# One whole transpose for the ninth key block, in place of two 64-row pieces

## The chip, the cores and the metric

One core of a Trainium2 chip runs the whole kernel. The metric is device time in microseconds (us) of one execution; of several runs the median is taken. The engines named below are TensorE (PE in the profile, with its weight loads as PEld), VectorE (DVE), ScalarE (ACT), GpSimd (POOL) and SyncE (SP), which issues the transfers.

## What is computed

Attention with queries pooled by two, then two feed-forward layers over the 1152 rows that it leaves. The change is in the attention alone. All data is float32.

```python
q_pool = q.reshape(B, H, S // 2, 2, D).mean(axis=3)       # B 2, H 8, S 1152, D 64
scores = D ** -0.5 * q_pool @ k.transpose(0, 1, 3, 2)     # 576 queries x 1152 keys
attn = exp(scores - max) / (sum + 1e-9)
x = (attn @ v)                                            # -> 1152 rows x 512
x = moe(x)        # x @ w_in, a rational function, @ w_out
out = moe2(x)     # RMS norm, silu gate, value, @ w_out
```

## The kernel before

**Tiles.** A pair of heads has 2 x 576 queries, cut into nine tiles of 128 queries (the fifth holds 64 of each head). Eight pairs give 72 tiles. A tile's scores are 128 queries by 1152 keys in one PSUM tile of three banks (`hid`; there are two of them, taken in turn: even tiles have one, odd tiles the other). Banks 0 and 1 hold 512 keys each, bank 2 the last 128, the ninth key block.

**A tile's steps.** TensorE computes the scores (line 782): `AB` is the part in banks 0 and 1, `C` the part in bank 2. VectorE takes the row maximum (line 811), ScalarE the exponential into `p` in SBUF (line 817). TensorE transposes `p` back into the same three banks (line 833), in pieces of 64 queries by 128 keys that use 64 rows of the array: pieces of queries 0 to 63 go to bank 0, those of queries 64 to 127 to bank 1, so that the two halves of the array work side by side. Three copies bring the banks to `pt` in SBUF (line 865 where ScalarE does it, 868 where VectorE does). Then `av` multiplies `pt` by the values (line 937). The scores of the tile after next need the same banks, so `AB` waits for the copies of banks 0 and 1, and `C` for that of bank 2.

**The ninth block.** It belongs in bank 2 for both halves. The piece of the upper queries goes there first, ahead of the other 16 pieces (`f_T`, 17 pieces). The piece of the lower queries is an operation of its own, `T2` (`f_T2`), which waits for the copy of bank 0; only after it is bank 2 copied.

**The other work in this stretch.** TensorE also transposes the next heads' `k` and `q` (`prep`, line 730) and the reciprocal sums (`rx`, lines 970 and 984), which take the whole 128 x 128 array. VectorE, ScalarE and GpSimd copy those results out, and prepare the weights of the feed-forward layers (`wc`, `wraw`, `spill`).

**Order.** Every step is an `Op` with a cost in ns. A list scheduler, `order`, writes the program from these costs, the keys and the dependencies, and chooses the engine of a step that may run on several (`op_any`). On TensorE the attention's steps are held in a row written by hand, `seq`: for tiles a and b of a couple it was AB(a), T2 of the couple before's b, C(a), AB(b), C(b), five steps of `av`, T(a), T(b), T2(a). `prep` and `rx` are put in between by the scheduler. The costs say 560 for `T` and 60 for `T2`; switching between row pieces, column pieces and the whole array is charged 100 between steps.

Of the kernel before, what the change touches and what calls it, by code (L numbers as in the profile page):

```python
# [19 lines left out]
def attention_moe_moe2_kernel(  # L20
# [18 lines left out]
    nc = tc.nc  # L39
    B, H, S, D = q.shape  # L40
# [25 lines left out]
    def T(tag, shape, dtype=F32, space=None):  # L66
        pool(tag, BUFS.get(tag, 1), space)
        return pools[tag].tile(shape, dtype, tag=tag, name=tag)
# [7 lines left out]
    ident = T("ident", [128, 128])  # L76
# [367 lines left out]
    PE, DVE, ACT, POOL = "PE", "DVE", "ACT", "POOL"  # L444
# [86 lines left out]

    after = mybir.DependencyInfo(mybir.DependencyClass.Sync, mybir.DependencyReason.DATA)

    def banked(accesses, g, ins, also=None):

        ins = ins.ins
        for o in range(3):
            for other in accesses[o]:
                if other.engine != ins.engine:
                    if o != g and other is not also:  # L540
                        tc.declare_no_dep(ins, other, reason="another bank")
                    else:
                        tc.add_manual_dep(ins, other.name, after, reason="the same bank")
        accesses[g].append(ins)
# [7 lines left out]
    def bank_access(w, u, c, ins):  # L552
        if w == "in" and u in FINE or (w, u) in (("gate", 0), ("val", NU2 - 1)):
            banked(hid_bank.setdefault((w, u), [[] for _ in range(NC)]), c, ins)
# [71 lines left out]
    def op_any(ways, key, deps=(), bufs=()):  # L626
        eng, c, fn = ways[0]
        return Op(eng, c, key, fn, deps, bufs, ways[1:])
# [7 lines left out]
    bank = [[[] for _ in range(3)] for _ in range(2)]  # L636
# [123 lines left out]
    pt, pt_buf, pt_op, sums, sum_buf, sum_op, xt_ops, xt_buf, x_op = ({} for _ in range(9))  # L760

    def tile_ops(i):
        pr, t = divmod(i, NT)
        parts, dests = TILES[t]
        ps = s_ps[i % 2]
        key = i * TS
        e = {}
        nb, pb = Buf("nm"), Buf("p")
        if t == 0:
            sum_buf[pr] = Buf("sums")  # L770
        sb = sum_buf[pr]


        ORDER_QK = [[(1, 1, 0, 256), (0, 0, 0, 256), (1, 1, 256, 512), (0, 0, 256, 512)], [(0, 2, 512, 640)]]

        def f_qk(n_):
            fresh = {}
            for a, j, x0, x1 in ORDER_QK[n_]:
                rows = slice(64 * a, 64 * a + 64)
                c = x0 % 512  # L780
                for h, c0, to in parts:
                    ins = nc.tensor.matmul(  # L782
                        ps[to, j, c:c + x1 - x0],
                        lhsT=qT[2 * pr + h][rows, c0:c0 + to.stop - to.start],
                        rhs=kT[2 * pr + h][rows, x0:x1],
                        start=True,
                        stop=True,
                    )
                    banked(bank[i % 2], j, ins)
                    fresh.setdefault(j, []).append(ins.ins)  # L790
            for j in fresh:
                bank[i % 2][j][:] = fresh[j]

        deps, bufs = [], []
        for h, c0, to in parts:
            deps += kT_op[2 * pr + h]
            deps += [o for (x0, x1), o in qT_op[2 * pr + h] if x0 < c0 + to.stop - to.start and x1 > c0]
            bufs += kq_buf[2 * pr + h]
        o_qk = []
        for n_, (js, c) in enumerate((((0, 1), 870), ((2,), 220))):  # L800
            free = [o for j in js for o in lo_op.get((i - 2, j), ())]
            o_qk.append(Op(PE, c, key + n_, lambda n_=n_: f_qk(n_), [*deps, *free], bufs))
            o_qk[-1].mode = "rows"
        tile_pe[i] = {"AB": o_qk[0], "C": o_qk[1]}

        def scores():
            return ps.rearrange("p g n -> p (g n)")[:, 0:S]

        def f_red():
            e["nm"] = T("nm", [128, 1])  # L810
            nc.vector.tensor_reduce(out=e["nm"], in_=scores(), op=ALU.max, axis=AX.X, negate=True)  # L811

        def f_exp():
            if pr not in sums:
                sums[pr] = T("sums", [128, NT])
            e["p"] = T("p", [128, S])
            nc.scalar.activation(  # L817
                e["p"], scores(), AF.Exp, bias=e["nm"], scale=1.0, accum_out=sums[pr][:, t:t + 1]
            )

        o_red = Op(DVE, 1350, key + -2500, f_red, o_qk, [nb])
        o_exp = Op(ACT, 1430, key + 2400, f_exp, [o_red], [nb, pb, sb])
        o_red.chain = o_exp.chain = True
        sum_op.setdefault(pr, []).append(o_exp)

        NB = NKT - 1

        def one_T(r, j, also=None):  # L830
            g, c = (2, 64 * r) if j == NB else (r, 64 * j)
            rows = slice(64 * r, 64 * r + 64)
            ins = nc.tensor.transpose(ps[:, g, c:c + 64], e["p"][rows, 128 * j:128 * j + 128], ident[rows, rows])  # L833
            banked(bank[i % 2], g, ins, also)

        def f_T():
            one_T(1, NB)
            for j in range(NB):
                one_T(0, j)
                one_T(1, j)  # L840

        def f_T2():
            one_T(0, NB, e["copied"].ins)


        OUTS = [(0, slice(0, NB), 0), (1, slice(0, NB), 1), (2, slice(NB, NKT), None)]

        def f_out(n_, copy):
            g, js, half = OUTS[n_]
            src = ps[:, g, 0:64 * NB if half is not None else 128]  # L850
            for h, o, s0, n in dests:
                if (pr, h) not in pt:
                    pt[pr, h] = T("pt", [128, NKT, SQ])
                to = pt[pr, h][:, js]
                if half is None:
                    banked(bank[i % 2], g, copy(to[:, 0, o:o + n], src[:, s0:s0 + n]))
                elif s0 <= 64 * half < s0 + n:
                    o_ = o + 64 * half - s0
                    ins = copy(to[:, :, o_:o_ + 64], src.rearrange("p (j n) -> p j n", n=64))
                    banked(bank[i % 2], g, ins)  # L860
                    if g == 0:
                        e["copied"] = ins

        def by_act(to, src):
            return nc.scalar.activation(to, src, AF.Copy)  # L865

        def by_dve(to, src):
            return nc.vector.tensor_copy(to, src)  # L868

        o_T = Op(PE, 560, key, f_T, [o_exp], [pb])  # L870
        o_T.mode = "rows"
        for h, *_ in dests:
            if (pr, h) not in pt_buf:
                pt_buf[pr, h] = Buf("pt")
        for n_ in range(3):
            half = OUTS[n_][2]
            hs = [h for h, o, s0, n in dests if half is None or s0 <= 64 * half < s0 + n]
            w = 64 * NB if half is not None else 128
            n2 = 150 * (len(hs) - 1)
            done = op_any(  # L880
                [(ACT, 70 + 1.09 * w + n2, lambda n_=n_: f_out(n_, by_act)), (DVE, 80 + 1.16 * w + n2, lambda n_=n_: f_out(n_, by_dve))],
                key + 3300 + 300 * n_, [o_T if half is not None else o_T2], [pt_buf[pr, h] for h in hs],
            )
            done.chain = True
            if n_ == 0:
                o_T2 = Op(PE, 60, key + 300, f_T2, [done], [pb])
                o_T2.mode = "rows"
                tile_pe[i].update(T=o_T, T2=o_T2)
            lo_op[i, OUTS[n_][0]] = [done]
            for h in hs:  # L890
                pt_op.setdefault((pr, h), []).append(done)
# [126 lines left out]
    tile_pe, av_ops = {}, []  # L1018
    AV2 = 5

    def attention():
        Op(PE, 213 * WARM, -1e6, f_warm)
        for i in range(len(heads)):
            head_ops(i)
        for i in range(NP * NT):
            tile_ops(i)
            if i % NT == NT - 1:
                pair_ops(i // NT)


        seq = []
        n = NP * NT
        for i in range(0, n, 2):
            a, b = tile_pe[i], tile_pe[i + 1]
            was = tile_pe.get(i - 1)
            seq += [a["AB"], *([was["T2"]] if was else []), a["C"], b["AB"], b["C"]]
            for _ in range(AV2):
                if av_ops and av_ops[0][0] < i - AVLAG:
                    seq.append(av_ops.pop(0)[1])
            seq += [a["T"], b["T"], a["T2"]]  # L1040
        seq.append(tile_pe[n - 1]["T2"])
        for x, y in zip(seq, seq[1:]):
            y.deps.append(x)

# [480 lines left out]
```

## Time and profile before

| | |
|---|---|
| three runs, median (lowest to highest) | 719.26 us (718.44 to 719.62) |
| profiled execution, its span | 719.1 us |
| attention, first transpose of `p` to the feed-forward's first product | 12.0 to 269.2 us of the span |
| TensorE busy over the span | 691.1 us (96%) |
| VectorE, ScalarE, GpSimd busy | 544.7, 392.6, 262.3 us |

The profiled execution is 0.2 us under the median of the runs, so a sum in its microseconds can be read against either. The profile counts an instruction as busy from its issue to its end; matmuls overlap one another, so that a busy TensorE is not a full one, and times between starts say more than busy shares. A product of float32 operands shows as two matmuls, a transpose as one.

### The profile page before, as it was taken

The numbers are of one execution on the slowest core, as the hardware profiler recorded it, in microseconds if no ns is written. First come the engines' busy times: TensorE is split into PE (matmuls) and PEld (weight loads), VectorE is DVE, ScalarE is ACT, GpSimd is POOL, SyncE is SP. The second block draws the span as 40 slices with busy tenths as digits, with TensorE's granted clock in tenths as the row PEclk, the third lists the DMA queues.
The fourth block names the chain that finished last, engine by engine and source line by source line (L and its number), as shares of the span: only waits on it lengthen the run. The fifth ranks groups of instructions, "written<-read, shape, count | busy, mean of one in ns | idle before, by whom it ended". The sixth has DMA issues, their size and how long they took to land.

```text
span 719.1 us, 13053 instructions
## 1 busy us (share of the span) xinstructions
PE 691.1 (96%) x5257; PEld 599.5 (83%) x5257; DVE 544.7 (76%) x732; ACT 392.6 (55%) x614; POOL 262.3 (36%) x245
## 2 busy tenths in 40 slices
PE   7999999999999999899999999998999999999997
PEld 6676767767676768789999999997999899989996
DVE  5599998999889883998996967958768146845844
ACT  4566767777777774988745655344334223402210
POOL 3022355566655554222222233155345033503500
PEclk9799999999999999999999999999999999999999
DMA  7333346574644525223104104010224212420103
GB/s 214 99 117 104 115 134 202 169 233 164 223 147 155 180 103 176 89 88 118 60 30 151 55 0 147 30 31 0 88 89 139 68 58 72 134 88 29 60 1 131
DMA packets 51596, 77.13 MB, mean 107 GB/s; under 512 B 4176, under 2 KB 33872, under 8 KB 51536
## 3 DMA queue, kind: packets, MB, share of 16 engines
q1 hardware_dynamic: 51536, 76.30, 32.8%
q8 instruction: 41, 0.67, 0.4%
q14 instruction: 19, 0.16, 0.1%
HBM read 61.87 MB, written 14.42 MB: 106 GB/s over the span
## 4 chain that ended last, share of the span: by engine, by line
PE 80%; DVE 10%; ACT 3%; issue 3%; DMA 2%; POOL 1%; SPq 0%; DVEq 0%; POOLq 0%; ACTq 0%
PE hid L525 31%; PE accp L525 23%; PE hid L782 9%; PE av L937 8%; PE hid L833 5%; PE prep L730 2%; DVE pt L868 2%; DVE nm L811 2%; ACT p L817 1%; DVE acc L1323 1%; DMA wraw<-in_moe_w_gate_dram 1%; DMA wraw<-in_moe_w_out_dram 1%; DVE xt L619 1%; DVE wc L184 1%; ACT pt L865 1%
## 5 line engine op out<-in xcount | busy, mean ns | idle before, releaser
L525 PE MATMUL hid<-x_hi,win_hi 128*128 128x384 f32 x480 | 161.5, 336 | 4.5 <-DVE m_p L1133 2.3
L525 PE MATMUL hid<-x_lo,win_hi 128*128 128x384 f32 x480 | 160.7, 335 | 0.6 <-DVE x_lo L1333 0.6
L525 PE MATMUL hid<-x_hi,win_lo 128*128 128x384 f32 x480 | 160.5, 334 | 0.0
L817 ACT ACTIVATE p<-hid,nm 128x1152 f32<-128x1152 f32 x72 | 87.8, 1220 | 32.9 <-DVE nm L811 32.3
L811 DVE TENSOR_REDUCE nm<-hid 128x1 f32<-128x1152 f32 x72 | 94.9, 1353 | 9.0 <-PE hid L782 7.4
L782 PE MATMUL hid<-kT,qT 64*128 64x256 f32 (+3 forms) x800 | 99.7, 379 | 1.9 <-DVE pt L868 1.6
L525 PEld LDWEIGHTS hid<-x_hi,win_hi 128*128 128x128 f32 x480 | 90.2, 188 | 7.3 <-issue 4.5
L1175 POOL TENSOR_TENSOR g_lo<-m_p,g_hi 128x1152 fp32r<-128x1152 f32 (+1 forms) x20 | 44.9, 2252 | 134.7 <-ACT g_hi L1172 96.4
L525 PEld LDWEIGHTS hid<-x_lo,win_hi 128*128 128x128 f32 x480 | 90.1, 188 | 1.8 <-DVE x_lo L1333 0.9
L525 PEld LDWEIGHTS hid<-x_hi,win_lo 128*128 128x128 f32 x480 | 90.1, 188 | 0.0
L782 PEld LDWEIGHTS hid<-kT,qT 64*128 64x128 f32 (+1 forms) x800 | 75.5, 182 | 12.0 <-DVE pt L868 3.4
L833 PEld LDWEIGHTS hid<-ident,p 64*128 64x128 f32 x1296 | 53.4, 141 | 36.3 <-ACT p L817 13.3
L833 PE MATMUL hid<-ident,p 64*128 64x64 f32 x1296 | 67.6, 231 | 10.7 <-ACT p L817 7.2
L865 ACT ACTIVATE pt<-hid 128x512 f32<-128x512 f32 (+2 forms) x135 | 57.0, 455 | 37.6 <-PE hid L833 36.5
L937 PE MATMUL av<-pt,vn 128*64 128x288 f32 x576 | 76.7, 411 | 0.0
L525 PE MATMUL accp<-g_hi,wout_hi 128*128 128x384 f32 x192 | 64.9, 338 | 2.8 <-ACT acc L1228 1.6
L868 DVE COPY pt<-hid 128x512 f32<-128x512 f32 (+1 forms) x89 | 50.4, 584 | 19.6 <-PE hid L833 19.2
L525 PE MATMUL accp<-g_lo,wout_hi 128*128 128x384 f32 x192 | 64.4, 335 | 0.1
L525 PE MATMUL accp<-g_hi,wout_lo 128*128 128x384 f32 x192 | 64.2, 334 | 0.0
L937 PEld LDWEIGHTS av<-pt,vn 128*64 128x64 f32 x576 | 38.6, 136 | 26.9 <-issue 2.7
L175 ACT ACTIVATE wc<-wraw 128x512 f32<-128x512 f32 x68 | 45.5, 671 | 24.6 <-POOL win_lo L208 14.7
L203 POOL TENSOR_SCALAR win_hi<-wc 128x512 fp32r<-128x512 f32 x23 | 15.8, 687 | 107.6 <-PE hid L525 90.8
(121 smaller groups left out, 1231.4 us busy)
## 6 DMA issues: line engine op xcount, KB each, us to landing
wraw<-in_moe_w_out_dram SPq DMA_DIRECT2D x28, 512.0 KB, 3.5
far<-spill SPq DMA_DIRECT2D x23, 512.0 KB, 3.5
wraw<-in_moe_w_in_dram SPq DMA_DIRECT2D x16, 512.0 KB, 3.9
wraw<-in_moe_w_gate_dram SPq DMA_DIRECT2D x12, 512.0 KB, 3.5
wraw<-in_moe_w_val_dram SPq DMA_DIRECT2D x12, 512.0 KB, 4.2
kn<-in_k_dram SPq DMA_DIRECT2D x16, 288.0 KB, 3.9
vn<-in_v_dram SPq DMA_DIRECT2D x16, 288.0 KB, 3.0
qn<-in_q_dram SPq DMA_DIRECT2D x16, 256.0 KB, 3.6
```

What stands on the lines that cost most here:

```text
L175: nc.scalar.activation(c.bitcast(F32), wt["raw", n][:, :, 1].bitcast(F32), AF.Abs, scale=2.0**-112)
L203: eng.tensor_scalar(hi, w_float(n), 1.0, 1.0, op0=ALU.mult, op1=ALU.mult)
L525: ins = nc.tensor.matmul(dst, lhsT=a[x], rhs=b[y], start=first and i == 0 and p == 0, stop=last and i == n - 1 and p == 2,)
L730: seen(nc.tensor.transpose(ps[0:src.shape[1], at:at + 128], src, ident))
L782: ins = nc.tensor.matmul(ps[to, j, c:c + x1 - x0], lhsT=qT[2 * pr + h][rows, c0:c0 + to.stop - to.start], rhs=kT[2 * pr + h][rows, x0:x1], ...
L811: nc.vector.tensor_reduce(out=e["nm"], in_=scores(), op=ALU.max, axis=AX.X, negate=True)
L817: nc.scalar.activation(e["p"], scores(), AF.Exp, bias=e["nm"], scale=1.0, accum_out=sums[pr][:, t:t + 1])
L833: ins = nc.tensor.transpose(ps[:, g, c:c + 64], e["p"][rows, 128 * j:128 * j + 128], ident[rows, rows])
L865: return nc.scalar.activation(to, src, AF.Copy)
L868: return nc.vector.tensor_copy(to, src)
L937: nc.tensor.matmul(e["av", h][64 * c:64 * c + 64, 0:QW], lhsT=v_tile[2 * pr + h][:, KEYS[kt], :], rhs=pt[pr, h][:, kt, c * QW:(c + 1) * QW ...
L1175: eng.tensor_sub(g_(1), p_(), g_(0).bitcast(F32))
```

## The change

The ninth block is transposed as one 128 x 128 block into bank 2, at the head of the tile's transposes, followed by the 16 row pieces of the other blocks. `T2` is gone from the tile and from the hand-written row, and with it its wait for the copy of bank 0. `T` is now costed at 750.

```diff
-    def banked(accesses, g, ins, also=None):
+    def banked(accesses, g, ins):
...
-                    if o != g and other is not also:
+                    if o != g:
                         tc.declare_no_dep(ins, other, reason="another bank")
...
-        def one_T(r, j, also=None):
-            g, c = (2, 64 * r) if j == NB else (r, 64 * j)
-            rows = slice(64 * r, 64 * r + 64)
-            ins = nc.tensor.transpose(ps[:, g, c:c + 64], e["p"][rows, 128 * j:128 * j + 128], ident[rows, rows])
-            banked(bank[i % 2], g, ins, also)
-
         def f_T():
-            one_T(1, NB)
+            banked(bank[i % 2], 2, nc.tensor.transpose(ps[:, 2, 0:128], e["p"][:, 128 * NB:S], ident))
             for j in range(NB):
-                one_T(0, j)
-                one_T(1, j)
-
-        def f_T2():
-            one_T(0, NB, e["copied"].ins)
+                for r in range(2):
+                    rows = slice(64 * r, 64 * r + 64)
+                    ins = nc.tensor.transpose(
+                        ps[:, r, 64 * j:64 * j + 64], e["p"][rows, 128 * j:128 * j + 128], ident[rows, rows]
+                    )
+                    banked(bank[i % 2], r, ins)
...
-        o_T = Op(PE, 560, key, f_T, [o_exp], [pb])
+        o_T = tile_pe[i]["T"] = Op(PE, 750, key, f_T, [o_exp], [pb])
...
-                key + 3300 + 300 * n_, [o_T if half is not None else o_T2], [pt_buf[pr, h] for h in hs],
+                key + 3300 + 300 * n_, [o_T], [pt_buf[pr, h] for h in hs],
...
-            if n_ == 0:
-                o_T2 = Op(PE, 60, key + 300, f_T2, [done], [pb])
...
-            was = tile_pe.get(i - 1)
-            seq += [a["AB"], *([was["T2"]] if was else []), a["C"], b["AB"], b["C"]]
+            seq += [a["AB"], a["C"], b["AB"], b["C"]]
...
-            seq += [a["T"], b["T"], a["T2"]]
-        seq.append(tile_pe[n - 1]["T2"])
+            seq += [a["T"], b["T"]]
```

On TensorE, a couple of tiles late in the attention stood like this before. `hid_156` is the PSUM tile of tile a, `hid_157` that of tile b; `p_...` are their exponentials, `kT`/`qT` the operands of the scores.

```order
L937 MATMUL av_3231<-pt_2979,vn_2653 64x288 x10
L833 MATMUL hid_156<-ident_66,p_3238 128x64 x17
L833 MATMUL hid_157<-ident_66,p_3251 128x64 x17
L833 MATMUL hid_156<-ident_66,p_3238 128x64
L782 MATMUL hid_156<-kT1_2909,qT1_2947 128x256 x4
L833 MATMUL hid_157<-ident_66,p_3251 128x64
L782 MATMUL hid_156<-kT1_2909,qT1_2947 128x128
L782 MATMUL hid_157<-kT0_3148,qT0_3196 128x256 x4
L782 MATMUL hid_157<-kT0_3148,qT0_3196 128x128
L937 MATMUL av_3231<-pt_2979,vn_2653 64x288 x8
```

Now the same couple stands like this:

```order
L926 MATMUL av_3156<-pt_2944,vn_2592 64x288 x10
L831 MATMUL hid_156<-ident_66,p_3159 128x128
L835 MATMUL hid_156<-ident_66,p_3159 128x64 x16
L831 MATMUL hid_157<-ident_66,p_3174 128x128
L835 MATMUL hid_157<-ident_66,p_3174 128x64 x16
L782 MATMUL hid_156<-kT1_2838,qT1_2871 128x256 x4
L782 MATMUL hid_156<-kT1_2838,qT1_2871 128x128
L782 MATMUL hid_157<-kT0_3077,qT0_3128 128x256 x4
L782 MATMUL hid_157<-kT0_3077,qT0_3128 128x128
L926 MATMUL av_3156<-pt_2944,vn_2592 64x288 x8
```

The two single pieces (`T2`) are gone, and each run of row pieces has a whole block at its head. Over the attention the program changes 229 times between row pieces, column pieces and the whole array, where it changed 155 times; the scheduler also puts some of `prep` and `rx` elsewhere.

The scheduler divides the copies anew. On VectorE, the work between the maxima of one couple (the 25th) and the next stood like this before; `xt` is the copy of `av`'s result.

```order
L811 TENSOR_REDUCE nm_2639<-hid_157 128x1
L180 TENSOR_SCALAR wc_2614<-wc_2614 128x512
L223 SCALAR_TENSOR_TENSOR wc_2614<-wraw_2394,wc_2614 128x512
L868 COPY pt_2491<-hid_156 128x8x64
L619 TENSOR_SCALAR xt_2442<-av_2529 64x288 x2
L868 COPY pt_2491<-hid_157 128x8x64
L988 TENSOR_TENSOR xt_2442<-xt_2442,prep_2573 128x512
```

And now:

```order
L811 TENSOR_REDUCE nm_2578<-hid_157 128x1
L180 TENSOR_SCALAR wc_2553<-wc_2553 128x512
L223 SCALAR_TENSOR_TENSOR wc_2553<-wraw_2335,wc_2553 128x512
L619 TENSOR_SCALAR xt_2383<-av_2469 64x288
L861 COPY pt_2438<-hid_156 128x8x64
L861 COPY pt_2438<-hid_156 128x128
L861 COPY pt_2646<-hid_157 128x8x64
L977 TENSOR_TENSOR xt_2383<-xt_2383,prep_2537 128x512
```

One `xt` has gone to ScalarE, the other stands ahead of the copies, and bank 2 of tile a is copied between the two large copies. Over the whole program VectorE loses 5 copies of `xt`, 12 of `qT`, 4 sums of `q` (`qp`), 5 small copies of `kT`, 4 products of `xt` with `rxh` and 2 of `win_lo`; it gains one large copy of `kT` and 16 of `pt`, two of them large.

## Rows read from the trace of the kernel before

**Rows 1.** Windows: engines' busy time (instructions), granted clock, DMA share, GB/s.

```profile
12.00:269.20 257.20, 245.52 (x2793) 175.67 (x2793) 225.78 (x339) 187.44 (x357) 121.18 (x129) 0.98 0.48 154
269.20:719.10 449.90, 436.59 (x2409) 415.83 (x2409) 314.16 (x382) 200.86 (x252) 137.40 (x108) 1.00 0.24 77
```

**Rows 2.** Line 833: TensorE idle before it (us, times), by what ended it.

```profile
  ACT p L817: 20.5, 30
...
  DVE pt L868: 8.9, 25
  ACT pt L865: 3.9, 13
```

**Rows 3.** Timeline of TensorE, 231.5 to 242.6: start, us, operation, count, idle before.

```profile
231.80 1.34 PE L833 MATMUL hid<-ident,p 64*128 64x64 f32 x34
233.37 0.27 PE L833 MATMUL hid<-ident,p 64*128 64x64 f32 x1 [0.23 <-DVE pt L868]
233.37 1.19 PE L782 MATMUL hid<-kT,qT 64*128 64x256 f32 x8
234.41 0.22 PE L833 MATMUL hid<-ident,p 64*128 64x64 f32 x1
234.46 1.52 PE L782 MATMUL hid<-kT,qT 64*128 64x128 f32 x12
235.91 2.16 PE L937 MATMUL av<-pt,vn 128*64 128x288 f32 x16
238.01 0.66 PE L730 MATMUL prep<-ident,kn 128*128 128x128 f32 x4
238.59 1.68 PE L833 MATMUL hid<-ident,p 64*128 64x64 f32 x35
```

**Rows 4.** Timeline of VectorE, 231.5 to 240.

```profile
232.62 1.29 DVE L868 COPY pt<-hid 128x512 f32<-128x512 f32 x2 [0.65 <-PE hid L833]
...
234.94 2.62 DVE L811 TENSOR_REDUCE nm<-hid 128x1 f32<-128x1152 f32 x2
```

**Rows 5.** Timeline of ScalarE, 231.5 to 240.

```profile
232.61 0.60 ACT L865 ACTIVATE pt<-hid 128x512 f32<-128x512 f32 x1 [0.35 <-PE hid L833]
```

**Rows 6.** Timeline of TensorE, 122.9 to 128.

```profile
123.48 0.77 PE L833 MATMUL hid<-ident,p 64*128 64x64 f32 x17
124.19 0.32 PE L970 MATMUL av<-ident,rx 128*128 128x128 f32 x1
124.44 0.88 PE L833 MATMUL hid<-ident,p 64*128 64x64 f32 x18
125.05 1.19 PE L782 MATMUL hid<-kT,qT 64*128 64x256 f32 x8
```

**Rows 7.** Timeline of TensorE, 7.7 to 12.5: the first two tiles.

```profile
7.80 2.44 PE L782 MATMUL hid<-kT,qT 64*128 64x256 f32 x20 [0.25 <-ACT qT L616]
10.18 0.30 PE L730 MATMUL prep<-ident,kn 128*64 128x128 f32 x1
```

**Rows 8.** Timeline of TensorE, 187.5 to 196.

```profile
187.56 0.33 PE L970 MATMUL av<-ident,rx 128*128 128x128 f32 x1
187.82 1.37 PE L833 MATMUL hid<-ident,p 64*128 64x64 f32 x34
...
189.40 1.19 PE L782 MATMUL hid<-kT,qT 64*128 64x256 f32 x8
191.08 0.27 PE L833 MATMUL hid<-ident,p 64*128 64x64 f32 x1 [0.49 <-DVE pt L868]
```

**Rows 9.** Timeline of VectorE, 187.5 to 196.

```profile
189.38 0.93 DVE L619 TENSOR_SCALAR xt<-av 64x288 f32<-64x288 f32 x2
190.33 0.69 DVE L868 COPY pt<-hid 128x512 f32<-128x512 f32 x1
```

**Rows 10.** Groups of VectorE's instructions, 12 to 269.2: busy us, mean ns, idle before.

```profile
L619 DVE TENSOR_SCALAR xt<-av 64x288 f32<-64x288 f32 x30 | 13.7, 455 | 2.4 <-PE av L937 1.6
L619 DVE TENSOR_SCALAR qT<-prep 128x256 f32<-128x256 f32 (+1 forms) x24 | 11.4, 474 | 0.5 <-PE prep L730 0.5
```

More of the change, by code (lines that the diff above doesn't have):

```diff
@@ L860, in f_out @@
                     banked(bank[i % 2], g, ins)
-                    if g == 0:
-                        e["copied"] = ins
         def by_act(to, src):
@@ L881, in tile_ops @@
                 [(ACT, 70 + 1.09 * w + n2, lambda n_=n_: f_out(n_, by_act)), (DVE, 80 + 1.16 * w + n2, lambda n_=n_: f_out(n_, by_dve))],
-                key + 3300 + 300 * n_, [o_T if half is not None else o_T2], [pt_buf[pr, h] for h in hs],
+                key + 3300 + 300 * n_, [o_T], [pt_buf[pr, h] for h in hs],
             )
             done.chain = True
-            if n_ == 0:
-                o_T2 = Op(PE, 60, key + 300, f_T2, [done], [pb])
-                o_T2.mode = "rows"
-                tile_pe[i].update(T=o_T, T2=o_T2)
             lo_op[i, OUTS[n_][0]] = [done]
```

## The prediction

> **What bounds the kernel now.** I read the windows first. The attention takes 257 of 719 us; the feed-forward behind it is not touched. In the attention VectorE is busy 225.8 us (88%), ScalarE 187.4 us (73%) and TensorE 245.5 us by overlapping instructions [rows 1]. So no engine is full, and the question is what follows what. The timeline of one couple without anything in between shows it. The 34 row pieces of both tiles start at 231.80, and T2(a) and the next scores AB(a) start together at 233.37, 1.57 us later [rows 3]. The pieces themselves can't fill that. In another couple 18 of them reach to the next step in 0.61 us (124.44 to 125.05), so 17 take 0.58 and two neighbours 0.06 [rows 6]. What fills it are the copies of tile a. They start at 232.61 and 232.62, 0.82 us after the first piece, and VectorE's first needs about 0.65 of the 1.29 us for two [rows 4, 5]; with the signals between engines that is 233.37. From AB(a) to `av` it is 2.54 us, with T2(b) within, and from there to the next couple's pieces 2.68 us of `av` and `prep` without a wait [rows 3]. A couple is thus one loop on TensorE, with one regular gap: the wait for tile a's copies.
>
> **What the change does not give.** Line 833 waits 8.9 + 3.9 = 12.8 us for copies [rows 2]. That looks like the prize, but T2(a) and AB(a) start at the same moment, and AB(a) overwrites the banks that these copies read. With T2(a) gone, AB(a) waits for them in its place. I cost this removal at nothing.
>
> **A, the block at the head of tile a.** It delays the 16 pieces, hence the copies, hence AB(a). The trace has a whole transpose right ahead of row pieces: `rx` at 187.56 and the pieces at 187.82, 0.26 us; in the other couple 124.19 to 124.44, 0.25 us [rows 6, 8]. It replaces one row piece (0.06), so 0.19 us. By the new order 21 of the 36 first tiles come after `av` or scores: 21 x 0.19 = 4.0 us. The other 15 come after `prep` or `rx`, so they change mode as often as before and pay only for a longer step. Four `prep` and the change take 238.01 to 238.59 = 0.58 us; less the 0.25 for the last with its change, 0.11 each [rows 3], against 0.06: 15 x 0.05 = 0.7 us. A is +4.7 us.
>
> **B, the block at the head of tile b.** Pieces to `rx` take 0.71 us (123.48 to 124.19), 0.13 more than 17 pieces without a change; with the 0.25 behind it, a whole transpose among pieces costs 0.71 + 0.25 - 0.58 = 0.38 us, and 0.32 in place of a piece [rows 6]. Yet that couple reaches its next scores at 125.05, again 1.57 us after its first piece, as the couple without `rx` does [rows 3, 6]: the wait for tile a's copies covers it. The cover is thin. With A the copies are ready 1.57 + 0.19 = 1.76 us after the start, and the pieces alone then need 0.25 + 0.52 + 0.13 + 0.25 + 0.52 + 0.06 = 1.73. So 27 blocks that follow row pieces cost nothing; without cover they would cost 27 x 0.32 = 8.6 us. The nine that follow `prep` or `rx` pay 0.05 each. B is +0.5 us.
>
> **C, T2(b).** It stands between AB(a) and C(a). The first two tiles of the kernel have scores without it: 7.80 to 10.18, 2.38 us to the next mode [rows 7], against 2.54 us with it [rows 3]: 0.16 us. The step from T2(b) to C(a) alone is 0.05 us (234.41 to 234.46), the lower bound [rows 3]. I take 0.13, nearer the direct comparison: 36 x 0.13 = -4.7 us, between -1.8 and -5.8.
>
> **D, late copies.** In the couple at 187.82 T2(b) starts 1.68 us after AB(a) (189.40 to 191.08), not 1.04 as at 233.37 [rows 3, 8]: VectorE made two `xt` (0.93 us) before the copy of tile b, which ran from 190.33 to 191.02 [rows 9]. In the new order one `xt` is on ScalarE and the other ahead; b's copy follows a's directly but for the small bank-2 copy. A's copy, with A's 0.19, ends near 189.57; a small copy and 0.69 more make about 190.5, half a microsecond sooner, and C(a) no longer waits behind it. Two couples have this order: -1.0 us, between 0 and -2.
>
> **E, the load that moves.** The 5 `xt` and 12 `qT` that leave VectorE are 5 x 0.455 + 12 x 0.474 = 8.0 us [rows 10]. Two large copies at 0.69 [rows 9] come, and 14 small ones, each under half of that: 1.4 to 6 us. So 2 to 7 us less on the fullest engine, and more on ScalarE, for whose exponentials the pieces waited 20.5 us [rows 2]. I take -1.0, between -4 and +3.
>
> **The sum.** 4.7 + 0.5 - 4.7 - 1.0 - 1.0 = -1.5 us: 719.1 - 1.5 = 717.6 us, 0.2% under the median of the runs. Two terms of nearly five cancel; the sign hangs on the small ones. This case's own range is 715.5 to 719.5.
>
> **Rivals.** *All changes of mode are paid.* The program changes mode 229 times in place of 155. If the copies come earlier than I think, or the planner leaves nothing to wait for, all 74 count at 0.13 us (the 0.71 against 0.58 of [rows 6]), 9.6 us, and 72 longer steps at 0.05, 3.6 us; less C, D and E, 6.7: +6.5, 725.6 us. It decides from the point where AB(a) no longer waits for copies. Against it stands the pair of 1.57 us, with and without `rx` [rows 3, 6]. The Trainium skill, TensorEngine Tiling (Array Packing), Key Properties, says that changing the tiling mode, and not just the tile, drains TensorE; the trace agrees on the price of a change, 0.13 us, and by that rule alone the time would be this rival's.
>
> *T2(b) was nearly free.* If it cost only its 0.05 us step, since C(a) would often wait anyway, C is -1.8 in place of -4.7, and with nothing from D and E the sum is 4.7 + 0.5 - 1.8 = +3.4: 722.5 us. For it speaks that single step; against it the whole distance, 2.54 against 2.38.
>
> *VectorE's lateness was the larger part.* If D takes its full bound and E too (-2 and -4), the sum is 4.7 + 0.5 - 4.7 - 6 = -5.5: 713.6 us. For it speaks VectorE's 88%; against it that its large copies in the plain couple started as soon as the pieces ended (232.62, after an idle wait) [rows 4].
>
> *Nothing comes of it.* Where the maxima (234.94, straight after the scores) [rows 4] and exponentials pace the loop, both the delay and the saving on TensorE vanish in waits: 719.1 us.
>
> **How the numbers follow.** The forecast has 0.46, of which I give 0.24 to over 0.2% faster and 0.22 to less (0.2%, 1.4 us, is about what a measurement of this kernel can tell from no change); late VectorE 0.18, cheap T2(b) 0.18, all changes paid 0.12, nothing 0.06. Faster: 0.24 + 0.18 = 0.42; same: 0.22 + 0.06 = 0.28; slower: 0.18 + 0.12 = 0.30. The range goes from the third rival, 713.5, to just over the second, 723.0, and leaves out the first.
>
> **What the new profile should show.** In a plain couple, first block to AB(a) 1.76 us in place of 1.57, ended by a copy; block to first piece 0.25; AB(a) to `av` 2.38 to 2.41 in place of 2.54; in the couple of D, AB(a) to AB(b) about half a microsecond shorter. Line 782 now waits for copies, 833's successor for exponentials alone. The prediction is wrong if the 1.76 is over 1.85 or ends without a wait, if AB(a) to `av` stays at 2.5, or if the exponentials come late because ScalarE has more to do.

## The result and the profile after

The changed kernel takes 729.22 us (median of 4 runs, 727.58 to 729.74) against 719.15 us for the kernel before beside it: a ratio of 1.0124, 95% interval 1.0101 to 1.0146. It is slower by 1.2%, by 10 us. The forecast was 717.6 us, in a range of 713.5 to 723.0. The profiled execution has a span of 728.0 us against 719.1, so the profile shows 8.9 us of the loss.

A few names for what follows. `x` is the feed-forward's input; it and the weights are each kept as a `hi` and a `lo` part, and a product of `x` is one of the matmuls `x_hi` by `win_hi`, `x_lo` by `win_hi` and `x_hi` by `win_lo`. 36 of them make a hidden block, which fills the three banks of one `hid` tile; the blocks take the two `hid` tiles in turn. VectorE and ScalarE then work out the rational function from it (`m_u`, `m_p`, `m_q`), and `accp` are the products of its result with the output weights (`wout`). A mark such as "the 73rd product" counts products of `x` from the first one on: the 73rd is the first of the third hidden block.

The windows show first where the loss is not. The columns are those of [rows 1]; the stretch is cut where the first product of the feed-forward starts, at 268.22 us now and at 269.20 us before. The last head's products with `v` come behind that cut.

```profile
12.00:268.20 256.20, 249.46 (x2721) 178.90 (x2722) 214.86 (x321) 192.08 (x367) 121.88 (x131) 0.99 0.47 152
268.20:728.00 459.80, 441.27 (x2408) 420.37 (x2408) 318.14 (x386) 202.39 (x254) 138.93 (x110) 0.99 0.23 77
```

The attention ends 1.0 us sooner than before [rows 1], and VectorE has lost 10.9 us of work there (225.78 to 214.86) while ScalarE has gained 4.6. The feed-forward, with the same products in both kernels, got 9.9 us longer. TensorE alone, in three stretches of it (busy time and instructions, granted clock, DMA share, GB/s), of before:

```profile
268.20:300.00 31.80, 27.99 (x175) 1.00 0.39 133
300.00:340.00 40.00, 38.31 (x217) 1.00 0.32 105
340.00:362.00 22.00, 21.98 (x128) 1.00 0.15 50
```

and of after:

```profile
268.20:300.00 31.80, 26.02 (x139) 0.89 0.39 133
300.00:340.00 40.00, 39.73 (x227) 1.00 0.32 106
340.00:362.00 22.00, 18.07 (x94) 0.92 0.14 48
```

Two stretches have fewer products and a lower granted clock, the first and the third. The rest of the program, from the 361st product of `x` to the last matmul, takes 333.3 us in both. So there are two places to explain.

**The first place** is the seam, where attention hands over. TensorE's timeline there, of before; the last line is the 73rd product of `x`:

```profile
274.53 0.60 PE L984 MATMUL prep<-ident,rx 128*128 128x128 f32 x4
275.06 0.27 PE L833 MATMUL hid<-ident,p 64*128 64x64 f32 x1
275.26 4.59 PE L937 MATMUL av<-pt,vn 128*64 128x288 f32 x36
279.77 0.33 PE L970 MATMUL av<-ident,rx 128*128 128x128 f32 x1
...
289.68 0.41 PE L525 MATMUL hid<-x_hi,win_hi 128*128 128x384 f32 x1 [2.29 <-DVE m_p L1133]
```

and of after:

```profile
273.54 0.60 PE L973 MATMUL prep<-ident,rx 128*128 128x128 f32 x4
273.89 0.42 PE L525 MATMUL hid<-x_hi,win_hi 128*128 128x384 f32 x1
...
279.29 4.59 PE L926 MATMUL av<-pt,vn 128*64 128x288 f32 x36
283.81 0.33 PE L959 MATMUL av<-ident,rx 128*128 128x128 f32 x1
286.64 0.44 PE L525 MATMUL hid<-x_hi,win_hi 128*128 128x384 f32 x1 [2.50 <-DVE x_hi L619]
287.44 0.69 PE L525 MATMUL hid<-x_lo,win_hi 128*128 128x384 f32 x1 [0.36 <-DVE x_lo L632]
287.92 0.52 PE L525 MATMUL hid<-x_hi,win_lo 128*128 128x384 f32 x1
...
293.91 0.65 PE L525 MATMUL hid<-x_hi,win_hi 128*128 128x384 f32 x1 [2.90 <-DVE m_p L1120]
```

Before, the single piece `T2` at 275.06 is followed by the last head's products with `v` (`av`), and the second hidden block's first 30 products come behind them. They write the banks of the last tile, and of these bank 2 was still to be copied when `av` began at 275.26:

```profile
275.36 0.28 ACT L865 ACTIVATE pt<-hid 128x128 f32<-128x128 f32 x1 [5.16 <-PE hid L833]
```

After, these 30 stand ahead of `av`, from 273.89 to 279.2. So `av` ends 4.0 us later, and behind it only 12 products are left ahead of the third block, every one of which needs the last heads' `x`. ScalarE and VectorE show its way:

```profile
284.48 0.82 ACT L616 ACTIVATE xt<-av 64x288 f32<-64x288 f32 x2
```

```profile
285.33 0.69 DVE L977 TENSOR_TENSOR xt<-xt,prep 128x512 f32<-128x512 f32 x1 [8.05 <-ACT xt L616]
286.13 0.46 DVE L619 TENSOR_SCALAR x_hi<-xt 128x576 fp32r<-128x576 f32 x1
286.62 0.76 DVE L632 TENSOR_TENSOR x_lo<-xt,x_hi 128x576 fp32r<-128x576 f32 x1
```

That way is as long as before, but nothing covers it now. From the `rx` transpose behind `av` to the 73rd product it is 9.91 us before, with 42 products in between, and 10.10 us after, with 12. The way goes on through the first block's last products and their steps on VectorE, which free the third block's banks (`m_p`, in the last line of either timeline). What the 30 products had been covering is now bare: from the first product to the 73rd it takes 25.7 us in place of 20.5.

**The second place** is 60 us later:

```profile
349.88 0.34 PE L525 MATMUL accp<-g_hi,wout_lo 128*128 128x384 f32 x1
353.99 0.41 PE L525 MATMUL hid<-x_hi,win_hi 128*128 128x384 f32 x1 [3.78 <-issue]
354.24 0.34 PE L525 MATMUL hid<-x_lo,win_hi 128*128 128x384 f32 x1
...
355.53 0.52 PE L525 MATMUL hid<-x_hi,win_lo 128*128 128x384 f32 x1
355.85 0.52 PE L525 MATMUL hid<-x_hi,win_hi 128*128 128x384 f32 x1
...
358.73 0.36 PE L525 MATMUL hid<-x_hi,win_hi 128*128 128x384 f32 x1
```

The profile names no releaser for this wait ("issue"). Two things come late in it, the next block's weights and its banks. SyncE's queue and VectorE's timeline show them:

```profile
349.03 0.32 SPq L248 DMA_DIRECT2D win_hi<-far  x1
349.44 0.38 SPq L248 DMA_DIRECT2D win_lo<-far  x1
```

```profile
351.16 1.41 DVE L1127 SCALAR_TENSOR_TENSOR m_q<-m_u,absb,hid 128x1152 f32<-128x1152 f32 x1
352.49 1.40 DVE L1120 SCALAR_TENSOR_TENSOR m_p<-m_p,ncoef,hid 128x1152 f32<-128x1152 f32 x1
```

The fetch of the weights is issued when the previous block's last products have been made, and only six products with the output weights are left to fill the 2.5 and 2.9 us that its two halves take to land, until 352.3. The banks are free later still: VectorE reads them for the last time in the step at 352.49, which ends at 353.89, 0.10 us before TensorE starts again. A step of the next block (351.16) stands ahead of it. In all six profiles that have this place (after, its repeat, and e2, e9, e10 and e11 below) that step of VectorE ends 0.10 to 0.11 us before TensorE's start, and the weights have landed 1.0 to 1.7 us before it. So the fetch can explain the wait up to 352.3, and what ends it is VectorE. Behind it the steps of TensorE fall to 0.32 us, where they were 0.17.

The profile so far gives: -1.0 (attention) + 5.2 (first to 73rd product) + 4.7 (73rd to 361st, 91.9 to 96.6 us) = 8.9 us.

### The profile page after: what moved, and what is told of

The parts are those of the page before. It is cut to its first block, busy times and chain, and to the rows that moved or that the text cites. A ratio compares the mean times of both kernels' runs of the same rounds, so it can differ in the third digit from the quotient of the medians.

```text
span 728.0 us, 12911 instructions
## 1 busy us (share of the span) xinstructions
PE 700.6 (96%) x5185; PEld 607.9 (84%) x5185; DVE 537.4 (74%) x717; ACT 398.4 (55%) x624; POOL 264.7 (36%) x250
## 4 chain that ended last, share of the span: by engine, by line
PE 86%; DVE 8%; ACT 3%; issue 2%; POOL 1%; DVEq 0%
PE hid L525 31%; PE accp L525 22%; PE hid L782 11%; PE av L926 10%; PE hid L835 6%; PE prep L730 3%; PE hid L831 2%; ACT p L817 1%; DVE m_q L1127 1%; DVE acc L1310 1%; DVE nm L811 1%; ACT m_p L1114 1%; DVE pt L861 1%; PE prep L973 1%; DVE m_p L1148 1%
## 5 line engine op out<-in xcount | busy, mean ns | idle before, releaser
L525 PE MATMUL hid<-x_hi,win_hi 128*128 128x384 f32 x480 | 163.4, 340 | 10.4 <-issue 3.9
L525 PE MATMUL hid<-x_lo,win_hi 128*128 128x384 f32 x480 | 162.6, 339 | 1.0 <-DVE x_lo L1320 0.6
L525 PE MATMUL hid<-x_hi,win_lo 128*128 128x384 f32 x480 | 162.2, 338 | 0.0
L782 PE MATMUL hid<-kT,qT 64*128 64x256 f32 (+3 forms) x800 | 94.2, 377 | 0.6 <-ACT qT L616 0.2
L861 DVE COPY pt<-hid 128x512 f32<-128x512 f32 (+2 forms) x105 | 53.9, 540 | 21.2 <-PE hid L835 20.5
L858 ACT ACTIVATE pt<-hid 128x512 f32<-128x512 f32 (+2 forms) x119 | 51.7, 476 | 23.8 <-PE hid L835 21.8
L835 PE MATMUL hid<-ident,p 64*128 64x64 f32 x1152 | 51.8, 230 | 0.0
L1400 ACT ACTIVATE g_hi<-m_p 128x1152 fp32r<-128x1152 f32 (+1 forms) x14 | 14.4, 1032 | 65.1 <-DVE m_p L1395 65.1
```

What stands on the lines that cost most here:

```text
L525: ins = nc.tensor.matmul(dst, lhsT=a[x], rhs=b[y], start=first and i == 0 and p == 0, stop=last and i == n - 1 and p == 2,)
L782: ins = nc.tensor.matmul(ps[to, j, c:c + x1 - x0], lhsT=qT[2 * pr + h][rows, c0:c0 + to.stop - to.start], rhs=kT[2 * pr + h][rows, x0:x1], ...
L835: ins = nc.tensor.transpose(ps[:, r, 64 * j:64 * j + 64], e["p"][rows, 128 * j:128 * j + 128], ident[rows, rows])
```

## The experiments

Theory 1 is that the change itself is near neutral, and that the scheduler (`order`, the planner below), with the gate `T2` gone, made another order at the seam and, as a consequence, another one around 349 us, where I took the fetch of the weights for the cause. In the planner's code a step that changes TensorE's mode counts as starting `SWITCH` = 100 ns later, and only steps within 80 ns of the earliest are ranked by key; `av` has the mode "columns", a product none. As long as a product is ready, `av` is not looked at. Before, the second block's products waited for the copy of bank 2 behind `T2`, so `av` came first. The rivals: the 74 added changes of mode are paid wherever they show, or the moved copies delay the weights.

All medians; each ratio is to the kernel before measured beside it (719.30 us for e1, e2, e5 and e6; 719.48 for e7, e9, e10 and e11; 719.55 for e12, e13 and after again; 720.69 for e14). Then four marks counted in each profile, in us: the start of the first product of `x`, of the last `rx` transpose, and of the 73rd and the 361st product.

| kernel | us | ratio, 95% interval | 1st | rx | 73rd | 361st |
|---|---|---|---|---|---|---|
| before | 719.15 | | 269.2 | 279.8 | 289.7 | 381.6 |
| after | 729.22 | 1.0124 (1.0101 to 1.0146) | 268.2 | 283.8 | 293.9 | 390.5 |
| after, again | 728.20 | 1.0119 (1.0096 to 1.0141) | 264.9 | 280.5 | 290.6 | 387.2 |
| e1: after, old order at the seam | 719.68 | 1.0002 (0.9986 to 1.0018) | 265.9 | 276.2 | 287.0 | 380.0 |
| e2: before, new order at the seam | 732.12 | 1.0166 (1.0143 to 1.0188) | 269.8 | 286.2 | 296.3 | 392.9 |
| e7: e1, TensorE's swap alone | 724.58 | 1.0078 (1.0050 to 1.0107) | 266.4 | 282.0 | 292.7 | 385.1 |
| e13: after, other order later on | 722.81 | 1.0040 (1.0023 to 1.0057) | 266.0 | 281.6 | 291.7 | 383.1 |
| e9: after, the wait filled | 727.76 | 1.0116 (1.0094 to 1.0139) | 266.0 | 281.6 | 291.8 | 388.5 |
| e5: e1, blocks side by side | 717.36 | 0.9977 (0.9963 to 0.9991) | 263.5 | 273.9 | 284.6 | 376.6 |
| e6: e1, blocks last | 720.13 | 1.0007 (0.9990 to 1.0024) | 266.6 | 277.0 | 287.7 | 379.7 |
| e10: e5, `av` first | 715.56 | 0.9941 (0.9917 to 0.9965) | 264.2 | 270.9 | 282.0 | 376.2 |
| e11: before, `av` first | 720.31 | 1.0008 (0.9991 to 1.0026) | 266.9 | 273.9 | 285.0 | 380.0 |
| e12: e10, other order later on | 714.19 | 0.9929 (0.9906 to 0.9952) | 263.7 | 270.4 | 281.5 | 374.2 |
| e14: e11, other order later on | 715.47 | 0.9938 (0.9917 to 0.9960) | 266.0 | 272.9 | 284.0 | 374.7 |

Profiles of one and the same attention differ by up to 3.8 us in the mark of the first product, so the distances between marks say more than the marks.

### e1 and e2: the order at the seam, in either kernel

e1 makes the second block's products wait for the last `av` in the changed kernel; e2 makes the last `av` wait for them in the kernel before.

```diff
# e1, on the changed kernel
         free = [o for g in range(3) for o in lo_op[NP * NT - 2 + u, g]]
+        if u == 1:
+            free.append(av_ops[-1][1])
# e2, on the kernel before
+    for _, x in av_ops:
+        x.deps += [early_h[1][1][c][2] for c in (1, 2)]
     order(80)
```

> The changed kernel with one edit: the second hidden block's first 30 products (whose inputs are early) may not be put ahead of the last head's 18 products with v. Attention keeps whole blocks, pieces without a wait, and all changes of mode. Theory 1 (the loss is made at the seam: with nothing left to cover the way of the last heads' x, TensorE idles and then runs at the lower clock; the late fetch at 350 us is a follow-up of the changed planner times): 717.5 to 720 us, no idle stretch over 1 us and no steps of 0.32 us from 280 to 300 us. If only the first idle stretch goes and the late fetch stays: 723 to 725. Rival 1 (changes of mode or the whole blocks cost the 10 us, wherever they show): 727 to 730. Rival 2 (redistributed copies on VectorE and ScalarE delay the weights for the feed-forward): 727 to 730 as well, with the fetch at 349 us still late.

> The kernel before with one edit: the last head's 18 products with v must follow the second hidden block's first 30 products, as in the changed kernel. Attention is that of before, without a whole block. Theory 1: slower than before by 4 to 10 us (723 to 729), with an idle stretch of 2 to 3 us behind the last rx transpose and steps of 0.32 us after it. Rivals 1 and 2: 718.5 to 720, since nothing in attention differs from before.

e1 takes 719.68 us, a ratio of 1.0002: with whole blocks, 229 changes of mode and the new division of copies all in place, the loss is gone. e2 takes 732.12 us: without any of them it is there, and more. Up to the seam TensorE's instructions in e1 are those of after, one for one, and in e2 those of before. That settles it for the order at the seam and against both rivals. One expectation on e1 was wrong: there is still a wait behind the seam, 3.1 us ahead of the 73rd product.

```profile
276.22 0.33 PE L959 MATMUL av<-ident,rx 128*128 128x128 f32 x1
...
286.99 0.41 PE L525 MATMUL hid<-x_hi,win_hi 128*128 128x384 f32 x1 [3.13 <-DVE m_p L1122]
```

It is the tail of the same 10 us way (10.8 here), which 42 products cover but for 3 us (2.3 in the kernel before). e2 shows the picture of after, with 26.5 us from the first to the 73rd product:

```profile
286.19 0.33 PE L970 MATMUL av<-ident,rx 128*128 128x128 f32 x1
289.01 0.67 PE L525 MATMUL hid<-x_hi,win_hi 128*128 128x384 f32 x1 [2.50 <-DVE x_hi L619]
...
296.28 0.66 PE L525 MATMUL hid<-x_hi,win_hi 128*128 128x384 f32 x1 [3.08 <-DVE m_p L1135]
```

### e7 and e13: the two places apart

e7 keeps the plan of e1 on all other engines and only issues the 30 products ahead of `av` on TensorE. e13 keeps the swap and moves the keys of the products with the output weights a little, so that another order is planned later on.

```diff
# e7, on e1
+    early = [x for c in range(NC) for x in early_h[1][1][c][:4 if c == 0 else 3]]
...
+    def f_swap():        # in place of the first av step's function
+        for f in fns:    # the 30 products' functions, taken from their own steps
+            f()
+        late[0]()
...
# e13, on the changed kernel
-        y1 = [k1[g[-1]] + 3 * P1 for g in g1]
+        y1 = [k1[g[-1]] + 3.1 * P1 for g in g1]
```

> e1 with one thing moved back: on TensorE alone the 30 products stand ahead of the last head's 18 products with v, as in the changed kernel; everything behind that place, the fetches of weights and the other engines' order among them, is e1's. Theory 1 splits the 9.5 us into two: the uncovered way of the last heads' x with the lower clock behind it (4 to 6 us), and the late fetch of weights at 349 us with its own fall of the clock (4 to 6 us), which hangs on the order that was planned for the time after. Then 723 to 726 us, with no idle stretch between 340 and 360 us. If the late fetch follows from the swap itself: 728 to 731. If only the planned order behind it costs: 719 to 720.

> The changed kernel with those keys at 3.1 steps: the swap at the seam and all of attention stay, the order changes from some 150 products later on. If the second place (4.1 us idle at 349.9 us and the slow steps behind it) is a matter of the order planned there: 4 to 6 us less than the changed kernel, 723 to 725.5, with the first place unchanged. If the fetch is late for another reason: 728 to 730.

e7 is 4.9 us above e1, with 26.3 us from the first to the 73rd product (21.1 in e1) and, as in e1, no idle stretch between 340 and 360 us. e13 is 6.4 us below after (5.4 below its repeat, measured beside it) and 0.2 below the range expected, with the first place as it was (25.7 us) and the second gone, in the window of 340 to 362 us:

```profile
340.00:362.00 22.00, 22.00 (x128) 1.00 0.21 73
```

So the swap costs about 5 us at the seam, and the order planned behind it another 5. The second does not follow from the swap: with e7's and e13's orders it is not there.

### e9: is it the clock?

e9 adds zero to a bank 12 times (`zcol` is a column of zeros) where TensorE waits in after, so that it does not stand idle.

```diff
                     nc.tensor.transpose(e["av", 1][:, 384:512], ...)
+                    for _ in range(12 if pr == NP - 1 else 0):
+                        ins = nc.tensor.matmul(env["in", 1][:, 2, 0:128], lhsT=ones,
+                            rhs=zcol.to_broadcast([128, 128]), start=False, stop=False)
```

> The changed kernel with 12 additions of zero (128x128 products, an operand of zeros) behind the last rx transpose, in the idle stretch of 2.5 us; no other engine is touched. If the slow steps behind the stretch (0.32 us at 286.6 to 290.7) come from the idle time ahead of them, they take 0.17 us: 1.5 to 3.5 us less than the changed kernel, 726 to 728. If they are slow because their inputs arrive slowly, or if the clock falls whatever TensorE does: 729 to 730.

```profile
281.72 2.84 PE L963 MATMUL hid<-zcol,ones 128*128 128x128 f32 x24
284.38 0.44 PE L527 MATMUL hid<-x_hi,win_hi 128*128 128x384 f32 x1
...
287.02 0.34 PE L527 MATMUL hid<-x_hi,win_lo 128*128 128x384 f32 x1
291.83 0.66 PE L527 MATMUL hid<-x_hi,win_hi 128*128 128x384 f32 x1 [4.48 <-DVE m_p L1127]
```

(Each addition leaves two records.) From 285.45 on the products now follow each other every 0.17 us, so the slow steps did come from the idle time ahead of them. But the next wait grew from 2.90 to 4.48 us, and the 73rd product comes 10.3 us after `rx`, no sooner. From the first product to the 73rd it is 25.8 us, as in after. The median, 727.76 us, lies in the range I had expected, but the gain that the range stood for isn't there: the ratio is 1.0116, and that of after 1.0124 and 1.0119. So ahead of the 73rd product the lower clock costs nothing: the chain on VectorE and ScalarE ends last anyway. Behind it nine more steps of after are slow, from 294.36 on, and eight in e9; what those cost this run does not tell.

### e5 and e6: the whole blocks' place

In e5 the block of tile a goes behind its pieces, next to the block of tile b; in e6 both go behind.

```diff
# e5, on e1 (e6: the block last in either tile)
+        def f_block():
+            banked(bank[i % 2], 2, nc.tensor.transpose(ps[:, 2, 0:128], e["p"][:, 128 * NB:S], ident))
+
         def f_T():
-            banked(bank[i % 2], 2, nc.tensor.transpose(ps[:, 2, 0:128], e["p"][:, 128 * NB:S], ident))
+            if i % 2 == 1:
+                f_block()
             for j in range(NB):
...
+            if i % 2 == 0:
+                f_block()
```

> e1 with the whole block of tile a behind its pieces, that of tile b still ahead of them: the two whole blocks of a couple stand side by side, two changes of mode fewer in each couple, and bank 0 and 1 of tile a are complete 0.2 us sooner. If the copies of tile a set the start of the next scores and the exponentials have room: first T row to AB(a) 1.86 -> 1.65 to 1.75 us, 2 to 6 us less than e1. If the exponentials or VectorE's reductions set the couple's length: within 1 us of e1, and the gain shows as a longer wait ahead of T.

> e1 with the whole block behind the pieces in both tiles: as many changes of mode as in e1, but the first two banks complete 0.2 us sooner in each tile. If the position counts (copies of bank 0 and 1 sooner): near e5. If the two spared changes of mode count: e6 equals e1 and e5 is below both by 35 x 2 x 0.1 = 7 us at most. If neither: all three within 1 us.

Both expectations had the changes of mode wrong. Counted over the attention they are 229 in e1, 206 in e5 and 251 in e6, since a block behind pieces and ahead of scores adds two changes where a block behind `prep` or `rx` had cost none. e5 is 2.3 us below e1, e6 level with it (0.45 above), and e5 2.8 below e6. Over 35 couples the distance from the first row of T to AB(a) sums to 70.5 us in e5, 73.8 in e1 and 73.9 in e6. Sooner banks alone would have made e6 as fast as e5, which it isn't. If the changes are all, the 23 spared come to 0.10 us each, and the 45 between e5 and e6 to 0.06. That in e6 sooner banks pay for the 22 more changes is possible and was not told apart, so the price of a change is known only to lie near 0.06 to 0.10 us.

### e10, e11, e12 and e14: a better seam

If 10 us of way have to be covered, `av` should come as early as it can. e10 (on e5) and e11 (on before) let only the first 9 products go ahead of it. e12 and e14 add other keys for the later order to e10 and e11.

```diff
# e10 on e5, e11 on the kernel before
-                o_rT = Op(PE, 120, key - 200, f_rT, [o_rx, last], [ab, rxb])
+                tile_pe["rT"] = o_rT = Op(PE, 120, key - 200, f_rT, [o_rx, last], [ab, rxb])
...
+    for u in FINE:
+        parts = [x for c in range(NC) for x in early_h[u][1][c]]
+        for x in parts[3 if u == 0 else 0:]:
+            x.deps.append(tile_pe["rT"])    # the transpose of rx behind the last av
     order(80)
# e12 on e10 (e14 on e11: 2.7)
-        y1 = [k1[g[-1]] + 3 * P1 for g in g1]
+        y1 = [k1[g[-1]] + 2.75 * P1 for g in g1]
```

> e5 with the last head's 18 products with v moved ahead: behind the first 9 products of the feed-forward instead of behind 30, so that the last heads' x is on its way 3.6 us sooner and 51 products cover it. Theory 1 goes on: the idle stretches behind the seam (2.6 and 1.4 us before, and slow steps where there are some) shrink, 2 to 5 us less than e5, 712 to 715. If the chains of the first hidden block, which then start 3.6 us later, hold TensorE instead: as e5, 717 to 718, with the idle time at another row.

> The kernel before with only that move of the 18 products with v. Tells how much of e10 is the seam and how much the whole blocks: by the profiles of e5 and e1 the blocks are worth 2 to 4 us in attention, so e11 should stand at e10 plus 2 to 4 us, 714 to 718. If the blocks are worth nothing: e11 equals e10.

> e10 with the keys of the products with the output weights 2.75 instead of 3 steps behind their block, so that another order is planned around 339 us, where e10 still idles 2.06 us ahead of products whose weights come from far. If that idle time is made by the order alone: 1 to 2 us less than e10, 713.5 to 714.5, without an idle stretch over 1 us from 330 to 360 us. If the fetch itself is the limit: as e10, 715 to 716, the stretch moved.

> e11 (the kernel before, without whole blocks, the last v products first) with the keys of the products with the output weights at 2.7 steps, so that the idle 3.05 us at 340.6 us goes as it went from e10 to e12. Tells what the whole blocks themselves are worth when both places are good. If they and their neighbourhood in e12 are worth the 2 to 4 us that the attention of e5, e10 and e12 is shorter by: 716 to 718.5. If the two places are all there is: 714 to 715, as e12. If the later place was not e11's loss: 720.

The seam does what was expected: 17.8 us from the first to the 73rd product in e10 and 18.0 in e11, where it was 21.1 and 20.5, and the 63 products behind `rx` fill the time:

```profile
266.42 4.59 PE L932 MATMUL av<-pt,vn 128*64 128x288 f32 x36
270.94 0.33 PE L965 MATMUL av<-ident,rx 128*128 128x128 f32 x1
...
282.03 0.33 PE L525 MATMUL hid<-x_hi,win_hi 128*128 128x384 f32 x1
...
341.24 0.41 PE L525 MATMUL hid<-x_hi,win_hi 128*128 128x384 f32 x1 [1.73 <-issue]
```

But the last line shows the second place again, ended as in after by VectorE's step and not by the weights, which had landed 1.0 us before. e10, at 715.56 us, thus stays just above the 712 to 715 expected, and in e11 it ate the whole gain: 95.1 us from the 73rd to the 361st product in place of 91.9, hence 720.31 us, a miss (714 to 718 expected). With the other keys it goes, to 92.7 us in e12 and 90.7 in e14. e12 is the fastest kernel of this study, 5.4 us below the kernel before measured beside it. e14, without a single whole block, stands at 0.9938 beside 0.9929: most of the gain is the two places. My expectation for e14 was 716 to 718.5. What the blocks are worth this does not tell: the two ratios differ by less than their intervals, but e14's later order is better by 2.0 us (90.7 against 92.7), while in the profiles e12's first product comes 2.3 us sooner. With the two blocks side by side (e5, e10, e12) the first product starts at 263.5 to 264.2 us, in all other profiles at 264.9 to 269.8.

### after, again

> The changed kernel itself, unedited, beside the other two on the same chip: 728 to 730 us, with both idle places as in its profile (2.8 and 3.2 us at 284 to 294, 4.1 us at 350).

728.20 us, and the same distances between marks (25.7 and 96.7 us) with an attention 3.3 us shorter in this execution. The two places are steady; the length of attention is what varies.

## Why the prediction was wrong

The step that failed stands in its third sentence, as an aside: "the feed-forward behind it is not touched". No product of the feed-forward was touched, but its order was, since the same planner places both; a dependency through the copy of bank 2 behind `T2` had been holding the second block back behind `av`. The sum had no term for it, and that term is +9.9 us in the profile: 5.2 at the seam and 4.7 later. The order of the changed program shows the 30 products ahead of `av`, so it could have been found.

The terms that the prediction did have:

- **The sum for attention, -1.5 us:** in the two profiles it is -1.0 [rows 1]. Over all profiles with either attention the first product starts at 268.0 us in the mean of four without blocks and at 266.2 in six with blocks of after's kind, 1.7 us sooner, with a scatter of twice that in each. The sum was about right, but by luck: costs and gains were both nearly twice as large.
- **A and B, +5.2 us:** over 35 couples the distance from T to AB(a) grew by 10.2 us, twice that. The plain couple shows it:

```profile
231.52 0.33 PE L831 MATMUL hid<-ident,p 128*128 128x128 f32 x1
231.78 0.71 PE L835 MATMUL hid<-ident,p 64*128 64x64 f32 x16
232.43 0.33 PE L831 MATMUL hid<-ident,p 128*128 128x128 f32 x1
232.69 0.71 PE L835 MATMUL hid<-ident,p 64*128 64x64 f32 x16
233.39 2.44 PE L782 MATMUL hid<-kT,qT 64*128 64x256 f32 x20
235.76 2.16 PE L926 MATMUL av<-pt,vn 128*64 128x288 f32 x16
```

```profile
232.64 0.69 DVE L861 COPY pt<-hid 128x512 f32<-128x512 f32 x1 [1.17 <-PE hid L835]
```

  Block to first piece is 0.26 us, as forecast. But first block to AB(a) is 1.87 us, not 1.76 (before 1.57 [rows 3]): VectorE's copy starts 1.12 us after the first row where it started 0.82 after it [rows 3, 4], 0.30 later and not 0.19. The prediction had named 1.85 as the point from which it is wrong, and a missing wait as another sign. That is there too: AB(a) shows no wait. TensorE's own steps fill the distance, 0.26 + 0.65 + 0.26 + 0.70 us, so the cover on which B was put at next to nothing is gone. Over the attention the scores of the new kernel wait for copies like this (us, times):

```profile
  DVE pt L861: 2.1, 9
```

  The forecast had the waits of 12.8 us for copies [rows 2] move there; most of them did not.
- **C and D, -5.7 us:** AB(a) to `av` is 2.37 us (2.38 to 2.41 forecast, 2.54 before [rows 3]). The two couples of D, measured from T to T, went from 7.98 to 7.30 and from 7.40 to 6.71 us, 0.7 each as against 0.5. From AB(a) to the last scores of the couple the sum over 35 couples fell by 8.8 us. So this term was too small as well, and the errors cancelled.
- **E, -1.0 us:** the rest of the loop, from the last scores to the next T, is 2.4 us shorter. The wait for exponentials did not grow with ScalarE's load, which was one of the signs of being wrong; it is 1.5 us less than before [rows 2]:

```profile
  ACT p L817: 19.0, 25
```

- **The rival "all changes of mode are paid", 725.6 us,** came nearest to the time and was wrong in its cause: e1 has all 229 changes and is level with before. Its costs were there, 10.2 us from T to AB(a) where it had 13.2 in all; its gains were too small, 6.7 us where 8.8 and 2.4 were measured. Its condition, AB(a) without a wait for copies, did come true in the plain couple. The Trainium skill, TensorEngine Tiling (Array Packing), Key Properties, says that changing the tiling mode drains TensorE. The runs agree that a change has a price, near 0.06 to 0.10 us each by e5 and e6, where [rows 6] gave 0.13.

## What to carry to other kernels

When one planner orders a whole program, a change has to be followed to where its section ends: compare the order of the instructions at the seam to the next stage, and ask which dependency that goes away had been holding something back. A serial way (here 10 us from the last products with `v` to the third hidden block) has to be covered by independent work that is queued behind its start and not ahead of it. Where a profile names no releaser for a wait, look for everything that the next instruction needs: here the late fetch was easy to see, and the banks came free later still. When a change slows a kernel far from the edit, put the old order back at the suspected place alone, and the new order into the old kernel; two runs then say more than any sum.

## What the runs showed of the chip

After the 4.1 us without work at 349.88 TensorE started again at full steps (0.17 us from 353.99 to 355.3) and only then fell to 0.32 us a step, from 355.53 to 358.73; the granted clock of 340 to 362 us is 0.92 for it. 0.32 us for 384 columns is the lower of the two levels, 1.2 GHz. So a wait's price in clock is paid behind the wait, some of it after work has resumed: here 10 steps of 0.15 us more, 1.5 us beside the 4.1. In e9 the filled wait raised the clock of 266 to 300 us from 0.90 to 0.95 and bought nothing up to the next mark, since the 73rd product waited for a chain on other engines that took as long.
